# Sparse attention and an MLP mixer on one core: row-tiled score visits of three steps over six PSUM banks, with all banks handed out by one planner

## The chip, the cores and the metric

The kernel runs on one core of one Trainium2 chip. The metric is the device time of one launch in microseconds (us). The kernel before took 253.83 us in the median of three runs (253.22, 253.83, 253.84).

The engines are TensorE (PE in the profile, its weight loads PEld), VectorE (DVE), ScalarE (ACT), GpSimd (POOL) and SyncE (SP). Matmul results go to PSUM, which has eight banks of 512 fp32 values per partition; everything else lies in SBUF.

## The reference

Attention over 4 batches, 8 heads, 768 positions and 64 channels per head, with a block mask (blocks of 32: neighbours, first and last block, and three sampled blocks per row of blocks). Its output is the input of an MLP mixer, first over positions, then over channels.

```python
scores = (q @ k.T) / sqrt(64)                  # per batch and head, 768 x 768
scores = where(mask, scores, -1e9)
attn = exp(scores - max) / (sum(...) + 1e-9)
x = (attn @ v)                                 # heads side by side: 4 x 768 x 512
h = relu(x.T @ w_tok1) @ w_tok2                # over positions: 768 -> 256 -> 768
u = x + h.T
h2 = relu(u @ w_ch1) @ w_ch2                   # over channels: 512 -> 1536 -> 512
out = u + h2                                   # fp32
```

## The kernel before

All matmuls are in bf16. Two heads make a pair; there are 16 pairs (four per batch). A pair's scores are computed transposed, keys on the partitions, in nine steps: three groups of 256 queries (t) by three groups of 256 keys (jj). A step is four matmuls into one PSUM tile of two banks, one bank per head, then one exp over 128 x 1024 values on ACT, and, from pair 5 on, one product with the 0/1 mask on DVE. For pairs 0 to 4 the mask is part of the matmul (88 rows: 64 channels and 24 mask rows). From pair 5 on the matmuls have 64 rows; head 0 lies on partitions 0 to 63 and head 1 on 64 to 127, so the two heads' matmuls use different rows of the array and run side by side. Such a stretch of 64-row matmuls is called a visit here.

```python
def scores(s, done, rel):
    p, t, jj = s
    P.take("ps", rel)
    P.take("et", et_rel[s])
    ps = psS.tile([128, 2, 512], FP32, tag="ps", name=f"ps{p}_{t}_{jj}")
    n = p % NV
    for i in range(2):
        for hd in range(2):
            rows, h = (slice(0, 88), hd) if p < NT0 else (slice(64 * hd, 64 * hd + 64), 0)
            nc.tensor.matmul(                                             # L707
                out=ps[:, hd, 256 * i : 256 * i + 256],
                lhsT=ktb[n][rows, h, 256 * jj + 128 * i : 256 * jj + 128 * i + 128],
                rhs=qtb[n][rows, h, 256 * t : 256 * t + 256],
                start=(i == 0), stop=(i == 1),
            )
    ...
        nc.scalar.activation(out=et[:, :, :], in_=ps[:, :, :], func=AF.Exp, scale=0.125)   # L717
    ...
    if p >= NT0:                                                          # NT0 = 5
            nc.vector.tensor_tensor(                                      # L725
                out=ets[s][:, :, :].rearrange("k h (i q) -> k h i q", i=2),
                in0=ets[s][:, :, :].rearrange("k h (i q) -> k h i q", i=2),
                in1=free(mask[:, 2 * jj, 256 * t : 256 * t + 256], 0, [[0, 2], [S, 2], [1, 256]]),
                op=ALU.mult,
            )
```

The product with v (the "PV" matmuls, L797) uses the exp tile as weights: eight matmuls of 65 columns per step (64 channels and a column of ones, for the sum). After the three steps of a group of queries DVE takes the reciprocal of the sums (L811) and scales (L812). Then come the mixer's matmuls: over positions (L877, L902, with 256 columns), over channels (first layer L1018, 384 columns, four per tile; second layer L1047, 512 columns, twelve per tile). A first-layer tile is evicted with a relu by ACT (L839) or DVE (L841), whichever the planner finds free, a second-layer tile by DVE with an add (L1059).

The instructions' order is not found on the chip. While the kernel is being built, a planner steps through its own model of the engines and decides what PE, ACT, DVE and SP do next; streams have priorities (scores first, then PV, then transposes and mixing). An instruction is emitted when its inputs and buffers would be free. PSUM is divided among three pools: two score tiles of two banks each (`psS`), one bank for the attention output (`psO`), three banks for transposes and mixing (`psM`).

```python
psS = ctx.enter_context(tc.tile_pool(name="psS", bufs=2, space=bass.MemoryType.PSUM))
psO = ctx.enter_context(tc.tile_pool(name="psO", bufs=1, space=bass.MemoryType.PSUM))
psM = ctx.enter_context(tc.tile_pool(name="psM", bufs=3, space=bass.MemoryType.PSUM))
...
def qk_stream():
    todo = list(steps)
    while todo:
        s = todo.pop(0)
        ...                                # p < NT0: one step at a time
        visit = [s]
        if s != (NT0, 0, 0) or len(todo) % 2:
            visit.append(todo.pop(0))
        ...
        n = len(visit)
        yield (
            420.0 if n == 1 else 650.0, [e for x in visit for e in qk_deps(*x)],
            [("ps", n), ("et", n)], emit, None,
        )
```

So from pair 5 on a visit has two steps (the very first has one), and it is emitted when both score tiles are free.

Of the kernel before, what the change touches and what calls it, by code (L numbers as in the profile page):

```python
# [50 lines left out]
class Planner:  # L51
# [13 lines left out]
    def __init__(self, slots):  # L65
        self.now = 0.0
        self.free_at = {"pe": 0.0, "act": 0.0, "dve": 0.0, "sp": 0.0}
        self.streams = []
        self.ops = []
        self.count = 0  # L70
        self.slots = {tag: [Ev(0.0)] * n for tag, n in slots.items()}
        self.exp_pending = 0
# [6 lines left out]
    def op(self, engines, cost, deps, emit, prio=5, lat=60.0, tags=()):  # L79
        done = Ev()  # L80
        self.ops.append((prio, self.count, engines, cost, deps, emit, done, lat, tags))
        self.count += 1
        return done

# [7 lines left out]
    def when(self, deps, tags=()):  # L92
        t = 0.0
        for d in deps:
            if d.t is None:
                return None
            t = max(t, d.t)
        for tag, n in tags:
            ts = sorted(e.t for e in self.slots[tag] if e.t is not None)
            if len(ts) < n:  # L100
                return None
            t = max(t, ts[n - 1])
        return t
# [77 lines left out]
def kernel(  # L181
# [12 lines left out]
    nc = tc.nc  # L194
# [9 lines left out]
    NET = 7  # L204
# [7 lines left out]
    psS = ctx.enter_context(tc.tile_pool(name="psS", bufs=2, space=bass.MemoryType.PSUM))  # L212
    psO = ctx.enter_context(tc.tile_pool(name="psO", bufs=1, space=bass.MemoryType.PSUM))
    psM = ctx.enter_context(tc.tile_pool(name="psM", bufs=3, space=bass.MemoryType.PSUM))
# [10 lines left out]
    P = Planner({"ps": 2, "po": 1, "pm": 3, "et": NET, "a_t": 2, "o": 3, "rc": 2,  # L225
                 "uT": 3})
# [98 lines left out]
    idle_ps = psS.tile([128, 2, 512], FP32, tag="ps", name="ps_idle")  # L325

    def idle_mm(n=512):
        nc.tensor.matmul(  # L328
            out=idle_ps[:, 0, 0:n], lhsT=free(one[:, 0:1], 0, [[0, 128]]),
            rhs=free(one[:, 0:1], 0, [[0, n]]), start=True, stop=True,  # L330
        )
# [68 lines left out]
    def first_turn(nm, lo, n):  # L400
        t = psM.tile([128, n, 128], BF16, tag="pm", name=f"t{nm}first{lo}")
        for c in range(n):
            nc.tensor.matmul(  # L403
                out=t[:, c, :], lhsT=lay0[nm][:, lo + c, :, :].rearrange("p h d -> p (h d)"),
                rhs=ident[:, :], start=(c == 0), stop=(c == n - 1), is_transpose=True,
            )
        return t
# [8 lines left out]
    def e2_mm(t, pool, tag):  # L416
        ps = pool.tile([128, 256], FP32, tag=tag, name=f"pm_e2_{t}")
        nc.tensor.matmul(
            out=ps[R, :], lhsT=t2add[R, :], rhs=indf[:, 256 * t : 256 * t + 256],
            start=True, stop=True,  # L420
        )
        return ps
# [10 lines left out]
    e2a = e2_mm(0, psO, "po")  # L433
    first_lay(acopy, "q", 0, 2)
    qt0 = first_turn("q", 0, 2)
# [4 lines left out]
    kt0 = first_turn("k", 0, 2)  # L440
# [3 lines left out]
    kt1 = first_turn("k", 2, 4)  # L444
# [23 lines left out]
    def first_rest():  # L468
        nc.sync.dma_start(out=ktb[1][R, :, :], in_=bandrows)
        for t in (1, 2):  # L470
            box, last, rel = {}, Ev(), Ev()

            def emit(t=t, box=box, rel=rel):
                P.take("pm", rel)
                box["t"] = first_turn("q", 2 * t, 2)
# [11 lines left out]
            def emit(t=t, ebox=ebox, erel=erel):  # L487
                P.take("pm", erel)
                ebox["t"] = e2_mm(t, psM, "pm")
# [10 lines left out]
        for n in range(1, NV):  # L500
            def spread(eng, n=n):
                if n > 1:
                    nc.sync.dma_start(out=ktb[n][R, :, :], in_=bandrows)
                if eng == "dve":
                    nc.vector.tensor_copy(out=qtb[n][R, :, :], in_=qtb[0][R, :, :])
                else:
                    nc.sync.dma_start(out=qtb[n][R, :, :], in_=qtb[0][R, :, :])

# [13 lines left out]
    def mask_stream():  # L522
        box, last, rel = {}, Ev(), Ev()

        def emit():
            P.take("pm", rel)
            box["m"] = psM.tile([128, NC, 24], FP32, tag="pm", name="pm_mask")
# [88 lines left out]
    def transposes(p):  # L616
# [15 lines left out]
        for nm, bufs, there in (("k", ktb, kT_there), ("q", qtb, qT_there)):  # L632
# [6 lines left out]
            for c in range(NC):  # L639
                def emit(nm=nm, c=c, box=box, rel=rel, raw=raw):  # L640
                    if c == 0:
                        P.take("pm", rel)
                        box["t"] = psM.tile([128, NC, 128], BF16, tag="pm", name=f"t{nm}{p}")
# [52 lines left out]
    et_rel = {s: Ev() for s in steps}  # L696

    def scores(s, done, rel):
        p, t, jj = s
        P.take("ps", rel)  # L700
        P.take("et", et_rel[s])
        ps = psS.tile([128, 2, 512], FP32, tag="ps", name=f"ps{p}_{t}_{jj}")
# [12 lines left out]
        def exp(eng):  # L715
            et = sbw.tile([128, 2, 512], BF16, tag="et", bufs=NET, name=f"et{p}_{t}_{jj}")
            nc.scalar.activation(out=et[:, :, :], in_=ps[:, :, :], func=AF.Exp, scale=0.125)  # L717
            ets[s] = et
            P.exp_pending -= 1

        ev = P.op(("act",), {"act": 948.0}, [done], exp, prio=0, lat=80.0)
        alias(rel, ev)
        if p >= NT0:
            def cut(eng):
                nc.vector.tensor_tensor(  # L725
                    out=ets[s][:, :, :].rearrange("k h (i q) -> k h i q", i=2),
                    in0=ets[s][:, :, :].rearrange("k h (i q) -> k h i q", i=2),
                    in1=free(mask[:, 2 * jj, 256 * t : 256 * t + 256], 0, [[0, 2], [S, 2], [1, 256]]),
# [3 lines left out]
            ev = P.op(("dve",), {"dve": 695.0}, [ev, mask_there], cut, prio=5)  # L732
        alias(et_there[s], ev)
# [6 lines left out]

    def qk_stream():
        todo = list(steps)
        while todo:
            s = todo.pop(0)
            p, t, jj = s
            yield lambda p=p: (p, 1) in qT_there
            if p < NT0:
                done, rel = Ev(), Ev()
                yield (
                    436.0, qk_deps(*s), [("ps", 1), ("et", 1)],  # L750
                    lambda s=s, done=done, rel=rel: scores(s, done, rel), done,
                )
# [4 lines left out]
            visit = [s]  # L757
            if s != (NT0, 0, 0) or len(todo) % 2:
                visit.append(todo.pop(0))
            yield lambda p=visit[-1][0]: (p, 1) in qT_there  # L760
            evs = [(Ev(), Ev()) for _ in visit]

            def emit(visit=visit, evs=evs):
                for n, (x, ev) in enumerate(zip(visit, evs)):
                    scores(x, *ev)
                    ev[0].t = P.now + 330.0 + 230.0 * n + P.PE_LAT + P.SEM

            n = len(visit)
            yield (
                420.0 if n == 1 else 650.0, [e for x in visit for e in qk_deps(*x)],  # L770
                [("ps", n), ("et", n)], emit, None,
            )
            for x, ev in zip(visit, evs):
                if x[1:] == (2, 2):
                    alias(qk_done[x[0]], ev[0])

    def pv_stream():
        for s in steps:
            p, t, jj = s
            done = et_rel[s]  # L780

            def emit(s=s, done=done):
                p, t, jj = s
                b, pb = p // 4, p % 4
                et = ets.pop(s)
                if jj == 0:
                    rel = Ev()
                    P.take("po", rel)
                    po_of[p, t] = (
                        psO.tile([128, 2, 2, 65], FP32, tag="po", name=f"po{p}_{t}"), rel  # L790
                    )
                po, rel = po_of[p, t]
                va = vaug[p % NV]
                for i in range(2):
                    for hd in range(2):
                        for c in range(2):
                            nc.tensor.matmul(  # L797
                                out=po[:, hd, c, :],
                                lhsT=et[:, hd, 256 * i + 128 * c : 256 * i + 128 * c + 128],
# [27 lines left out]
            yield 236.0, [et_there[s], va_there[p], ones_there[p % NV]], [("po", 1)] if jj == 0 else [], emit, done  # L827
            if (t, jj) == (2, 2):
# [18 lines left out]
    def new_uT(b):  # L847
        P.take("uT", st[b]["uT_rel"])
        st[b]["uT"] = sbw.tile([128, 2, NC, 2, 128], BF16, tag="uT", bufs=3, name=f"uT{b}")
# [15 lines left out]
    def tok(b, g):  # L865
# [5 lines left out]
        for t in range(2):  # L871
            for sc in range(NC):
                def emit(t=t, sc=sc):
                    if t == 0 and sc == 0:
                        P.take("pm", rel)
                        box["pm"] = psM.tile([128, 2, 256], FP32, tag="pm", name=f"pm_tok1_{b}_{g}")
# [15 lines left out]
        for s2 in range(3):  # L892
            last, rel, ubox = Ev(), Ev(), {}
            for i in range(2):
                for t in range(2):
                    def emit(i=i, t=t, s2=s2, rel=rel, ubox=ubox):
                        if i == 0 and t == 0:
                            P.take("pm", rel)
                            ubox["pm"] = psM.tile(
                                [128, 2, 256], FP32, tag="pm", name=f"pm_tok2_{b}_{g}_{s2}"  # L900
                            )
# [21 lines left out]
    def tok_first(p):  # L923
# [5 lines left out]
        for t in range(2):  # L929
            for sc in range(NC):  # L930
                def emit(t=t, sc=sc):
                    if t == 0 and sc == 0:
                        P.take("pm", rel)
                        box["pm"] = psM.tile([128, 2, 128], FP32, tag="pm", name=f"pm_tok1_0_{p}")
# [15 lines left out]
        for s3 in range(2):  # L950
            last, rel, ubox = Ev(), Ev(), {}
            for i in range(3):
                for t in range(2):
                    def emit(i=i, t=t, s3=s3, rel=rel, ubox=ubox):
                        if i == 0 and t == 0:
                            P.take("pm", rel)
                            ubox["pm"] = psM.tile([128, 3, 128], FP32, tag="pm", name=f"pm_tok2_0_{p}_{s3}")
# [16 lines left out]
        for sc in range(NC):  # L974
            def emit(sc=sc, rel=rel, tbox=tbox):
                if sc == 0:
                    if p == 0:
                        new_uT(0)
                    P.take("pm", rel)
                    tbox["pt"] = psM.tile([128, NC, 128], BF16, tag="pm", name=f"pm_ut_0_{p}")  # L980
# [20 lines left out]
    def ch(b, pool, tag):  # L1001
# [4 lines left out]
        for cc in range(12):  # L1006
            for sh in range(2):
                last, rel, pbox = Ev(), Ev(), {}
                for dmc in range(4):
                    first = dmc == 0  # L1010
                    def emit(cc=cc, sh=sh, dmc=dmc, rel=rel, pbox=pbox):
                        if dmc == 0:
                            P.take("pm", rel)
                            pbox["pm"] = psM.tile([128, 512], FP32, tag="pm", name=f"pm_ch1_{b}_{cc}_{sh}")
# [8 lines left out]
                    tags = [("pm", 1)] if first else []  # L1023
# [16 lines left out]
        for sc, lo, n in parts:  # L1040
            last, rel, pbox = Ev(), Ev(), {}
            for cc in range(12):
                def emit(sc=sc, cc=cc, lo=lo, n=n, rel=rel, pbox=pbox):
                    if cc == 0:
                        P.take("pm", rel)
                        pbox["pm"] = psM.tile([128, DM], FP32, tag="pm", name=f"pm_ch2_{b}_{sc}_{lo}")
# [4 lines left out]
                yield n / 2.4 + 2.5, [rc_there[cc, sc // 3], ch2_there[cc // 3]], [("pm", 1)] if cc == 0 else [], emit, last if cc == 11 else None  # L1051
# [47 lines left out]
    def ch_stream():  # L1099
        for b in range(B):  # L1100
            yield from ch(b, psM, "pm")
# [88 lines left out]
```

The softmax here doesn't subtract the row's maximum and nothing guards it: scores larger than these inputs give would overflow.

## Time and profile before

One execution was profiled; its span is 253.1 us.

| engine | busy, us | share | instructions |
|---|---|---|---|
| PE (matmul) | 247.9 | 98% | 2807 |
| ACT | 177.9 | 70% | 225 |
| DVE | 167.0 | 66% | 372 |
| PEld (weight loads, beside PE) | 163.4 | 65% | 2807 |

The granted clock of TensorE is full (1.0) in the whole span. From 25 to 50 us, in pairs 0 to 4, ACT is busy for 24.75 of 25 us; from 75 to 100 us for 20.1, and DVE for 22.4. After 184 us no scores are left, and PE alone works through the rest of the mixer.

How to read it: the busy time of an engine is the union of its instructions' records. Matmuls overlap in the records and their ends are modelled, so the distance from one matmul's start to the next says more than its length. A group's line gives the source line, engine, operation, output and inputs by name with shapes, count, then busy time and mean length in ns, then the engine's idle time just before them and what ended it. A wait line reads "engine, line, waited for engine, line: total us, times, longest us". "Issue" is time for which the profile shows nothing waited for. In a timeline or in the chain of work that ended last, the first number is the start in us and the second the length.

### The profile page before, as it was taken

Reading aid. Unit: us, or ns where it says so; the run is one execution under the profiler, and the core shown is the slowest. Engines: PE = TensorE matmul, PEld = TensorE weight load, DVE = VectorE, ACT = ScalarE, POOL = GpSimd, SP = SyncE. Lnnn points to the kernel's source line nnn. Section 1 sums busy time; section 2 is a strip of 40 time slices with the busy share of each in tenths; the row PEclk is TensorE's granted clock in tenths of the full one; section 3 lists DMA queues with packets and bytes.
Section 4 is the critical chain, followed back from the end, with each engine's and each line's share of the span. In section 5 each row is a group of like instructions: output and inputs, shape, how many; then the busy total and the mean of one; then the engine's idle time right before and its main releaser. Section 6 shows DMA issues by size and latency. Waiting matters only on the chain.

```text
span 253.1 us, 6675 instructions
## 1 busy us (share of the span) xinstructions
PE 247.9 (98%) x2807; PEld 163.4 (65%) x2807; DVE 167.0 (66%) x372; ACT 177.9 (70%) x225; POOL 49.9 (20%) x86
## 2 busy tenths in 40 slices
PE   7999999999999999999999999999999999999994
PEld 3689999966666557556766765575576644566444
DVE  4885875788989888988889898888853012200222
ACT  5699999999888868778989787677665710277000
POOL 8845989477400000000000000000000000000000
PEclk9999999999999999999999999999999999999999
DMA  7999999999978531934153013114112012300132
GB/s 169 164 211 201 213 205 202 204 201 201 201 121 132 100 92 42 169 115 74 34 96 62 4 22 84 43 43 106 44 43 51 14 41 84 124 3 0 41 115 95
DMA packets 42462, 26.36 MB, mean 104 GB/s; under 512 B 23680, under 2 KB 38800, under 8 KB 42432
## 3 DMA queue, kind: packets, MB, share of 16 engines
q0 software_dynamic: 15104, 12.98, 32.4%
q1 hardware_dynamic: 26784, 12.56, 20.8%
q8 instruction: 22, 0.36, 0.6%
q10 hardware_dynamic: 544, 0.39, 0.5%
q14 instruction: 8, 0.07, 0.1%
HBM read 26.74 MB, written 6.29 MB: 131 GB/s over the span
## 4 chain that ended last, share of the span: by engine, by line
PE 96%; DMA 2%; ACT 1%; DVE 0%; SPq 0%; issue 0%
PE pm_ch L1018 25%; PE pm_ch L1047 25%; PE ps L707 19%; PE po L797 15%; PE pm_tok L902 3%; PE pm_tok L877 3%; DMA kf<-in_k_dram 2%; PE pm_tok L958 1%; PE pm_tok L935 1%; PE tk L649 1%; PE tq L649 1%; PE pm_ut L981 1%; ACT et L717 0%; PE ps_idle L328 0%; PE tkfirst L403 0%; PE tqfirst L403 0%
## 5 line engine op out<-in xcount | busy, mean ns | idle before, releaser
L717 ACT ACTIVATE et<-ps 128x1024 bf16<-128x1024 f32 x144 | 138.8, 1022 | 26.9 <-PE ps L707 25.9
L1018 PE MATMUL pm_ch<-uT,w_ch 128*128 128x384 bf16 x384 | 71.8, 326 | 0.0
L1047 PE MATMUL pm_ch<-w_ch,rc 128*128 128x512 bf16 (+2 forms) x312 | 70.4, 363 | 0.0
L725 DVE TENSOR_TENSOR et<-et,mask 128x1024 bf16<-128x1024 bf16 x99 | 63.9, 684 | 1.7 <-ACT et L717 1.7
L797 PEld LDWEIGHTS <-et 128*128 128x128 bf16 x1152 | 49.1, 97 | 15.7 <-issue 3.0
L707 PE MATMUL ps<-qtb,ktb 64*128 64x256 bf16 (+1 forms) x576 | 58.1, 273 | 0.5 <-ACT et L717 0.5
L797 PE MATMUL po<-vaug,et 128*128 128x65 bf16 x1152 | 55.4, 193 | 0.1
L839 ACT ACTIVATE rc<-pm_ch 128x384 bf16<-128x384 f32 x70 | 34.1, 493 | 26.3 <-PE pm_ch L1018 26.0
L1018 PEld LDWEIGHTS <-w_ch 128*128 128x128 bf16 x384 | 34.7, 97 | 21.4 <-issue 2.5
L1059 DVE TENSOR_TENSOR o<-pm_ch,x 128x512 f32<-128x512 f32 x23 | 15.8, 688 | 47.3 <-PE pm_ch L1047 47.2
L1047 PEld LDWEIGHTS <-rc 128*128 128x128 bf16 x312 | 27.4, 98 | 24.7 <-issue 1.5
L707 PEld LDWEIGHTS <-ktb 64*128 64x128 bf16 (+1 forms) x576 | 30.9, 96 | 15.6 <-issue 11.8
L812 DVE TENSOR_TENSOR x<-po,recip 128x256 bf16<-128x256 f32 x48 | 20.4, 424 | 1.7
L811 DVE RECIPROCAL recip<-po 128x4 f32<-128x4 f32 x48 | 8.7, 181 | 18.6 <-PE po L797 17.9
L841 DVE TENSOR_SCALAR rc<-pm_ch 128x384 bf16<-128x384 f32 x26 | 14.4, 554 | 2.8 <-PE pm_ch L1018 2.3
L910 DVE TENSOR_TENSOR x<-pm_tok,x 128x512 bf16<-128x512 f32 x18 | 12.0, 685 | 3.9 <-PE pm_tok L902 3.8
L902 PE MATMUL pm_tok<-a_t,w_tok 128*128 128x256 bf16 x72 | 10.7, 276 | 0.0
L877 PE MATMUL pm_tok<-x,w_tok 128*128 128x256 bf16 x72 | 9.7, 273 | 0.0
L902 PEld LDWEIGHTS <-w_tok 128*128 128x128 bf16 x72 | 7.6, 128 | 1.7 <-issue 1.1
L265 POOL DMA_DIRECT2D vraw<-in_v_dram x10 | 7.4, 738 | 3.3 <-DVE vaug L583 1.2
L877 PEld LDWEIGHTS <-w_tok 128*128 128x128 bf16 x72 | 6.5, 98 | 1.7 <-issue 0.8
L553 POOL COPY mask<-maskb 128x240 bf16<-128x240 bf16 (+1 forms) x18 | 7.4, 482 | 0.0
(93 smaller groups left out, 132.0 us busy)
## 6 DMA issues: line engine op xcount, KB each, us to landing
out_dram<-o SPq DMA_DIRECT2D x23, 256.0 KB, 2.0
w_ch<-in_moe_w_ch_dram POOLq DMA_DIRECT2D x8, 384.0 KB, 9.8
vraw<-in_v_dram POOLq DMA_DIRECT2D x10, 192.0 KB, 7.5
kraw<-in_k_dram POOLq DMA_DIRECT2D x9, 192.0 KB, 8.3
qraw<-in_q_dram POOLq DMA_DIRECT2D x9, 192.0 KB, 7.3
w_tok<-in_moe_w_tok_dram POOLq DMA_DIRECT2D x2, 384.0 KB, 10.3
qf<-in_v_dram POOLq DMA_DIRECT2D x4, 192.0 KB, 7.9
klay_first<-in_k_dram POOLq DMA_DIRECT2D x2, 192.0 KB, 8.3
```

The source lines that it names most:

```text
L707: nc.tensor.matmul(out=ps[:, hd, 256 * i : 256 * i + 256], lhsT=ktb[n][rows, h, 256 * jj + 128 * i : 256 * jj + 128 * i + 128], rhs=qtb[n] ...
L717: nc.scalar.activation(out=et[:, :, :], in_=ps[:, :, :], func=AF.Exp, scale=0.125)
L725: nc.vector.tensor_tensor(out=ets[s][:, :, :].rearrange("k h (i q) -> k h i q", i=2), in0=ets[s][:, :, :].rearrange("k h (i q) -> k h i q" ...
L797: nc.tensor.matmul(out=po[:, hd, c, :], lhsT=et[:, hd, 256 * i + 128 * c : 256 * i + 128 * c + 128], rhs=va[:, hd, 2 * jj + i, 0:65], star ...
L812: nc.vector.tensor_tensor(out=free(xs[b][:, pb // 2, 2 * t, 128 * (pb % 2) : 128 * (pb % 2) + 128], 0, [[64, 2], [256, 2], [1, 64]],), in0 ...
L839: nc.scalar.activation(out=o(), in_=i, func=AF.Relu)
L841: nc.vector.tensor_scalar(out=o(), in0=i, scalar1=0.0, scalar2=None, op0=ALU.max)
L877: nc.tensor.matmul(out=box["pm"][:, t, :], lhsT=w_tok1[:, sc, 128 * t : 128 * t + 128], rhs=xs[b][:, g, sc, :], start=(t == 0 and sc == 0) ...
L902: nc.tensor.matmul(out=ubox["pm"][:, i, :], lhsT=w_tok2[:, t, :, 2 * s2 + i], rhs=a_t[:, t, :], start=(i == 0 and t == 0), stop=(i == 1 an ...
L1018: nc.tensor.matmul(out=pbox["pm"][:, 0:384], lhsT=w_ch1[:, dmc, 128 * cc : 128 * cc + 128], rhs=st[b]["uT"][:, dmc // 2, 3 * sh : 3 * sh + ...
L1047: nc.tensor.matmul(out=pbox["pm"][:, 0:n], lhsT=box["rc"][:, cc, 128 * sc : 128 * sc + 128], rhs=w_ch2[:, cc, lo : lo + n], start=(cc == 0 ...
L1059: nc.vector.tensor_tensor(out=o[:, :].rearrange("p (g e) -> p g e", g=2), in0=pbox["pm"][:, :].rearrange("p (g e) -> p g e", g=2), in1=st[ ...
```

## The change

What it does:

- From pair 5 on the nine steps of a pair become three units of three steps (one group of queries each), and a visit is one unit: twelve matmuls in a row into six banks, in three pairs of two.
- The PSUM pools go. There is one PSUM tile with all eight banks, and the planner hands out bank numbers. Until the last scores of pair 4 the division is as before. From then on the scores have banks 0 to 5, emitted when all six are free, and the attention output and the mixing tiles share banks 6 and 7. Where neither is free, a free score bank is lent, if a rule (`lend`) finds that the next scores could not start soon anyway. After the last scores all eight banks serve the mixer.
- The exp tile holds a unit (three steps) and has its key blocks ahead of the heads in memory, so that one product with the mask can cover two steps: per unit one over 2048 and one over 1024 values. There are three such tiles, in place of seven of one step.
- The transposed mixer inputs (uT) have two buffers in place of three. The order of two transfers at the start of the kernel is exchanged.

What it is for: fewer changes between row-tiled matmuls and full ones, fewer instructions on DVE, and PSUM banks that serve whichever work can use them.

The diff, cut to its core ("..." marks cuts; the remaining hunks replace pool tiles by `take_bank` or `in_bank` in the same way):

```diff
+    def sets(self, tag):
+        pairs = [(0, 1), (2, 3), (4, 5)]
+        if tag == "ps":
+            return pairs[: 2 if self.shared == 0 else 3], []
+        if tag == "unit":
+            return [(0, 1, 2, 3, 4, 5)], []
+        if self.shared == 0:
+            return [(6,)] if tag == "po" else [(4,), (5,), (7,)], []
+        return [(6,), (7,)], [(n,) for n in range(6)]
...
+    def bank(self, tag, release):
+        own, lent = self.sets(tag)
+        groups = [g for g in own if self.ready(g) <= self.now]
+        if not groups:
+            assert self.shared == 2 or self.lend(tag)
+            groups = [g for g in lent if self.ready(g) <= self.now]
...
-    NET = 7
+    NET = 3
...
-    psS = ctx.enter_context(tc.tile_pool(name="psS", bufs=2, space=bass.MemoryType.PSUM))
-    psO = ctx.enter_context(tc.tile_pool(name="psO", bufs=1, space=bass.MemoryType.PSUM))
-    psM = ctx.enter_context(tc.tile_pool(name="psM", bufs=3, space=bass.MemoryType.PSUM))
+    psum = ctx.enter_context(tc.tile_pool(name="psum", bufs=1, space=bass.MemoryType.PSUM))
+    banks = psum.tile([128, 8, 512], FP32, name="banks")
...
+    CUTS = ((0, 1), (2,))
...
-            et = sbw.tile([128, 2, 512], BF16, tag="et", bufs=NET, name=f"et{p}_{t}_{jj}")
-            nc.scalar.activation(out=et[:, :, :], in_=ps[:, :, :], func=AF.Exp, scale=0.125)
+                ets[p, t] = sbw.tile(
+                    [128, 3, 2, 2, 256], BF16, tag="et", bufs=NET, name=f"et{p}_{t}"
+                )
+            nc.scalar.activation(
+                out=ets[p, t][:, jj, :, :, :].rearrange("k i h q -> k h i q"),
+                in_=ps.rearrange("k h (i q) -> k h i q", i=2), func=AF.Exp, scale=0.125,
+            )
...
+            def cut(eng, lo=group[0], n=len(group)):
+                et = ets[p, t][:, lo : lo + n, :, :, :].rearrange("k j i h q -> k (j i) h q")
                 nc.vector.tensor_tensor(
+                    out=et, in0=et,
+                    in1=free(mask[:, 2 * lo, 256 * t : 256 * t + 256], 0,
+                             [[S, 2 * n], [0, 2], [1, 256]]),
                     op=ALU.mult,
                 )
...
+    UNSEEN, LATER = 2500.0, 1800.0
+    HOLD = {"pm": 1600.0, "po": 1800.0, "ch1": 1800.0, "ch2": 4000.0}
+
+    def lend(tag):
...
+        return P.now + HOLD[tag] <= max(ts) + LATER
...
-            yield (
-                420.0 if n == 1 else 650.0, [e for x in visit for e in qk_deps(*x)],
-                [("ps", n), ("et", n)], emit, None,
-            )
+            def emit(p=p, t=t, evs=evs, exps=exps):
+                P.take("et", et_rel[p, t])
+                order = sorted((0, 2, 4), key=lambda n: P.ready((n, n + 1)))
+                for jj, (done, rel) in enumerate(evs):
+                    queue.popleft()
+                    P.banks[order[jj]] = P.banks[order[jj] + 1] = rel
+                    scores((p, t, jj), order[jj], done, rel, exps)
+                    done.t = P.now + 330.0 + 230.0 * jj + P.PE_LAT + P.SEM
+                if not queue:
+                    P.shared = 2
+
+            yield 870.0, qk_deps(p, t, 0), [("unit", 1), ("et", 1)], emit, None
...
-                                lhsT=et[:, hd, 256 * i + 128 * c : 256 * i + 128 * c + 128],
+                                lhsT=et[:, jj, i, hd, 128 * c : 128 * c + 128],
...
-        st[b]["uT"] = sbw.tile([128, 2, NC, 2, 128], BF16, tag="uT", bufs=3, name=f"uT{b}")
+        st[b]["uT"] = sbw.tile([128, 2, NC, 2, 128], BF16, tag="uT", bufs=2, name=f"uT{b}")
```

## The prediction

> **What bounds the kernel now.** I read the page first (engines, chain, groups), then the waits, then the timeline of one stretch, where the cost of a visit can be measured. The first part of the page, and the engine line of the chain that ended last:
>
> ```profile
> PE 247.9 (98%) x2807; PEld 163.4 (65%) x2807; DVE 167.0 (66%) x372; ACT 177.9 (70%) x225; POOL 49.9 (20%) x86
> ...
> PE 96%; DMA 2%; ACT 1%; DVE 0%; SPq 0%; issue 0%
> ```
>
> TensorE (PE) is busy for nearly the whole span and is nearly the whole chain. Ends of matmuls are modelled, so 98% alone does not say that it streams all the time; the distances between starts do. The chain in order of time, after the last scores:
>
> ```profile
> 192.66 10.52 PE pm_ch L1018 x64
> 203.18 15.54 PE pm_ch L1047 x72
> 218.72 15.60 PE pm_ch L1018 x96
> ```
>
> 10.52/64 = 0.164 us and 15.60/96 = 0.1625 us for a matmul with 384 columns, 15.54/72 = 0.216 us for one with 512: no gap in the tail. Now the stretch with row-tiled scores (pairs 5 to 15, from about 51 to 184 us), PE's timeline; columns are start, length, engine and line, operation, shapes, count:
>
> ```profile
> 83.10 0.59 PE L1047 MATMUL pm_ch<-w_ch,rc 128*128 128x512 bf16 x2
> 83.62 0.61 PE L707 MATMUL ps<-qtb,ktb 64*128 64x256 bf16 x8
> 84.17 0.66 PE L797 MATMUL po<-vaug,et 128*128 128x65 bf16 x16
> 84.66 0.81 PE L1047 MATMUL pm_ch<-w_ch,rc 128*128 128x512 bf16 x3
> ```
>
> Read starts against starts. Two L1047 from 83.10 would end at 83.10 + 2 x 0.216 = 83.53; the visit starts at 83.62, so 0.09 us go at its entry. The eight score matmuls (64 rows; the two heads run side by side, so four pairs) occupy 84.17 - 83.62 = 0.55 us. A pair streams 256 columns, 0.107 us by the 512-column pitch halved, so four take 0.43; 0.12 are left at the first pair and the exit. **One visit thus costs about 0.20 us beside its streaming.** Sixteen L797 then take 84.66 - 84.17 = 0.49, or 0.031 each, without a gap. The individual starts of the stretch say the same at all visits but one (at 55 us): their edges add up to some 9.4 us, and everything else that is not streaming to some 0.5 us.
>
> The waits:
>
> ```profile
> ACT et L717 <- PE ps L707: 25.9, 40, 1.6
> PEld L707 <- issue: 11.8, 36, 0.4
> PE ps L707 <- ACT et L717: 0.5, 1, 0.5
> ```
>
> ScalarE (ACT) waits for scores (25.9 us); PE waits for an exp once in the whole run. So neither ACT nor VectorE (DVE) holds PE up. The second line is the visit edge seen from the weight loads: before scores of a visit they wait for "issue", 0.3 us each, not for data.
>
> ACT's part of a visit, from both timelines:
>
> ```profile
> 86.30 0.61 PE L707 MATMUL ps<-qtb,ktb 64*128 64x256 bf16 x8
> 88.97 0.61 PE L707 MATMUL ps<-qtb,ktb 64*128 64x256 bf16 x8
> ...
> 86.73 1.94 ACT L717 ACTIVATE et<-ps 128x1024 bf16<-128x1024 f32 x2 [0.73 <-PE ps L707]
> ```
>
> The first exp starts 0.43 us after the visit, two take 1.94 (one 1.02 by the groups, so the second starts 0.92 after the first), and the next visit comes 2.67 us after the last. PE had 2.67 us of work there, ACT needed 2.37.
>
> **What the Trainium skill says.** "TensorEngine Tiling (Array Packing)", section Key Properties: changing the tiling mode drains TensorE. The trace agrees in kind: the edges of a visit (64 rows in, 128 out) cost 0.20 us, while L1047, L797 and L1018 follow each other freely. The same page, section "Gotcha 1: PSUM Pressure": row tiles write to different banks; so a step holds two banks here, and three steps six of eight. "VectorE: DVE Perf Modes", section "The perf-mode tier table": tensor_tensor in bf16 takes 1224 ns for 2048 elements; this trace has only 1024 elements (684 ns), which implies a fixed share of 2 x 684 - 1224 = 144 ns, an estimate from that page and the row. "Perfetto Trace Analysis", section "Identifying the Most-Contended Engine", warns that matmul busy time doesn't measure the headroom; hence the start distances above.
>
> **The change, part by part.**
> 1. Visits. 99 row-tiled steps (11 pairs x 9). Before: one single and 49 doubles = 50 visits. After: 33 triples. The matmuls stay 2807, of the same shapes. 17 visits less x 0.20 us = **-3.4 us**, all on PE, which sets the end.
> 2. Masking. Instead of 99 products of 1024 elements, 33 of 2048 and 33 of 1024: 33 x 0.144 = 4.8 us less on DVE (estimate, from above). DVE is not on the chain: 0 us. The first step's product now waits for the second exp, 0.92 us later, but its weights are used in a later period (in the order of the built program the mixing products of a unit come after the next visit or later): 0 us.
> 3. exp. Same 144 instructions of 1024 elements, but the output is written in runs of 256 in another order. I know no reason for another duration: 0 us. Were it slower, pairs 0 to 4 would show it (rival C).
> 4. Attention buffers: 3 of three steps for 7 of one. The first step of a unit needs the products of seven steps earlier done, as before; the later ones less: 0 us. uT from 3 to 2: the third is wanted only when the first has long been read: 0 us.
> 5. Banks. Up to pair 4 the order of PE's instructions is the same as before until the last scores of pair 4. Then the scores get banks 0 to 5 and the rest 6 and 7, plus lent ones. Two effects can cost. (a) ACT: three exps need 0.43 + 2 x 0.92 + 1.02 = 3.29 us from a visit's start. From the built order I summed PE's work from each visit to the next (0.216, 0.1625, 0.109, 0.056, 0.031 us by kind, 0.84 for a triple visit): mostly 3.5 to 4.4 us, six to ten in some, but 2.66 once and 3.09 twice. There PE would come 0.63 + 0.2 + 0.2 = 1.0 us early. But each step of a visit waits only for the exp of its own two banks, so the first two steps can run and part of the wait is taken up: I put +0.5. (b) Mixing tiles: a first-layer tile streams 4 x 0.1625 = 0.65 us and its eviction takes 0.50 (ACT) to 0.55 (DVE); with two banks, one often held by the attention output, the next tile may wait some tenths. Lending and the PV matmuls in between cover most of it; +0.3, a guess.
> 6. Tail (after the last visit): only wide matmuls at full pitch before; eight banks instead of three change nothing, since none waited.
>
> Sum: 253.83 - 3.4 + 0.5 + 0.3 = 251.2; since planner and trace left only 0.5 us beside edges before, I lean slightly to the good side: **251.0 us**, 1.1% less.
>
> **Rivals.**
> A. *The round trip to ACT becomes the bound.* For: all six banks of a unit come from one set, so no scores can be made ahead while the exps run, and 3.29 us of ACT stand against periods of 3.5. Against: before, 2.37 stood against 2.66, the same margin, without a stall; per step the round trip shrinks from 1.19 to 1.10 us. If each visit came 0.2 us late, 33 x 0.2 = 6.6 us: 257.
> B. *Bank shortage for the mixing tiles.* For: three banks of their own become one or two. Against: lent banks. 0.1 us at each of some 50 first-layer tiles in this stretch would be +5 us: about 255.5.
> C. *exp gets slower by the other layout.* In pairs 0 to 4 ACT is as full as PE (24.75 of 25 us busy between 25 and 50 us), so 50 ns on 45 exps would be +2.3 us: 253. Nothing in the trace before speaks for it.
> D. *DVE's relief pays.* It would need PE to wait for DVE now; the waits show 1.5 us in all of weight loads after a masking product, 0.2 at most each, and PE's starts show no gap there: at most some tenths.
>
> **Range and chances.** The edges are the only loss of PE that the change touches, so 253.83 - 3.4 = 250.4 is about the best; with the spread of the runs (253.22 to 253.84) the low end is 250.0. The high end, 252.9, lets A, B or C take 2.5 of the 3.4. To be faster by over 2% (below 248.8) it would have to save 5.1 us, more than there is: 0.02. Slower by over 2% (above 258.9) needs A or B at full size: 0.05. Within 2%: 0.93.
>
> **What would show it.** Right: 33 groups of twelve score matmuls, each with about 0.2 us of edges; the weight loads' "issue" wait before scores at two thirds of 11.8 us; fewer us of ACT waiting for scores; the tail at 0.1625 and 0.216 us. DVE less busy by about 5 us with nothing gained from it. Wrong by A: PE waiting for ACT at scores, in many visits. By B: gaps ahead of the first-layer or second-layer matmuls that end with an eviction on DVE or ACT. By C: exp's mean above 1022 ns and gaps before 50 us. The prediction fails if the edge is not per visit but per score matmul, or if PE stalls spread over the stretch so that span minus streaming does not fall.

## The result and the profile after

The changed kernel took **252.22 us** in the median (252.14 to 252.35) against 253.83 us before: 1.6 us less, a ratio of 0.9943 with a 95% interval of 0.9926 to 0.996. That is inside the predicted range, at a bit more than half of the predicted gain.

The first part of the page of the kernel after, with the engine line of its chain:

```profile
PE 244.2 (98%) x2807; PEld 163.6 (65%) x2807; DVE 164.3 (66%) x339; ACT 176.4 (70%) x225; POOL 49.5 (20%) x86
...
PE 95%; DVE 2%; ACT 1%; issue 1%
```

PE is still nearly the whole chain, but DVE has entered it with 2%. That is the first sign of the loss.

Two spans must not simply be subtracted: the profiles have 253.1 and 250.4 us, 2.7 apart, while the timed runs differ by 1.6. The cure is an anchor, a point up to which both programs do the same. It is the last scores of pair 4. PE's timeline of the kernel before, then that of the kernel after:

```profile
50.15 0.60 PE L707 MATMUL ps<-qtb,ktb 88*128 88x256 bf16 x4
```

```profile
49.11 0.60 PE L764 MATMUL banks<-qtb,ktb 88*128 88x256 bf16 x4
```

1.04 us of the difference had arisen before, where PE's order is the same. The profiled execution of the kernel before took 254.8 us, 0.97 over its median, and that of the kernel after 252.14, close to its own; so this part belongs to the one execution and not to the change. From the anchor to the start of the last matmul the traces have 199.56 us before and 197.93 after: **1.63 us less**, as the timed runs say. Sorting the distances between PE's starts in this stretch, each less the streaming of its matmul (0.216 us for 512 columns, 0.1625 for 384, 0.109 for 256, about 0.03 for 65):

| from the last scores of pair 4 to the end, us | before | after | difference |
|---|---|---|---|
| entries and exits of row-tiled visits (50, 33) | 9.39 | 6.43 | -2.96 |
| inside the visits, beyond 0.107 per pair of heads | one stall of 0.2, 11 ns at each first pair | 11 ns at each first pair | -0.4 |
| gaps between full matmuls, over 25 ns each | 0.47 (6) | 2.46 (9) | +2.0 |
| small scatter | 0.24 | 0.04 | -0.2 |
| sum | | | -1.6 |

After one of the 33 visits the next matmul comes 0.21 us later than after the others; the table counts this with the exits, but it is a gap of the new kind:

```profile
114.26 0.42 DVE L904 TENSOR_TENSOR x<-banks,recip 128x256 bf16<-128x256 f32 x1
114.74 0.64 PE L889 MATMUL banks<-vaug,et 128*128 128x65 bf16 x16
```

These attention (PV) matmuls start 0.06 us after the scaling of the attention output before them has ended; in the built program both outputs have the same bank, 6. Counted so, the edges fell by 3.2 us and the gaps grew by 2.2.

So the edges gave what they should, and new gaps took more than half of it back. This is the largest, as PE's and DVE's timelines of the kernel after show it (in brackets: idle time before, and what ended it):

```profile
89.09 0.83 PE L764 MATMUL banks<-qtb,ktb 64*128 64x256 bf16 x12
89.85 0.60 PE L1132 MATMUL banks<-w_ch,rc 128*128 128x512 bf16 x2
90.29 0.89 PE L889 MATMUL banks<-vaug,et 128*128 128x65 bf16 x24
91.22 0.18 DVE L903 RECIPROCAL recip<-banks 128x4 f32<-128x4 f32 x1 [0.53 <-PE banks L889]
91.44 0.42 DVE L904 TENSOR_TENSOR x<-banks,recip 128x256 bf16<-128x256 f32 x1
91.92 0.81 PE L1132 MATMUL banks<-w_ch,rc 128*128 128x512 bf16 x3 [0.73 <-DVE x L904]
92.66 0.61 PE L764 MATMUL banks<-qtb,ktb 64*128 64x256 bf16 x8
```

A triple visit, two second-layer matmuls, then the 24 PV matmuls. They end streaming at 90.29 + 24 x 0.031 = 91.03; the next second-layer tile starts at 91.92, 0.89 us later. What it waits for is DVE's scaling of the attention output (L904). That instruction writes x, which L1132 doesn't read; what it frees is the PSUM bank of the attention output. The two banks outside the scores were that one and the one of the second-layer tile just finished, which DVE evicts only after the scaling. No score bank was lent: in the built program the new tile has bank 6, which the attention output held. So TensorE stood still for a bank, although ACT, the round trip of the scores and DVE's load were in order.

The other long gaps: 0.48 us at 99 us (position mixing waits for the relu of its own middle result, by DVE), 0.21 at 105 and 0.46 at 140 us (second-layer tiles again, the latter after L904 too), and some 0.1 to 0.2 us ahead of PV matmuls. The one at 105 us ends 0.05 us after another eviction, that of the second-layer tile before it, which had the same bank in the built program:

```profile
104.46 0.69 DVE L1144 TENSOR_TENSOR o<-banks,x 128x512 f32<-128x512 f32 x1 [0.35 <-PE banks L1132]
105.20 0.81 PE L1132 MATMUL banks<-w_ch,rc 128*128 128x512 bf16 x3
```

### The profile page after: what moved, and what is told of

The parts are those of the page before. It is cut to its first block, busy times and chain, and to the rows that moved or that the text cites. A ratio compares the mean times of both kernels' runs of the same rounds, so it can differ in the third digit from the quotient of the medians.

```text
span 250.4 us, 6599 instructions
## 1 busy us (share of the span) xinstructions
PE 244.2 (98%) x2807; PEld 163.6 (65%) x2807; DVE 164.3 (66%) x339; ACT 176.4 (70%) x225; POOL 49.5 (20%) x86
## 4 chain that ended last, share of the span: by engine, by line
PE 95%; DVE 2%; ACT 1%; issue 1%
PE banks L1132 25%; PE banks L1104 24%; PE banks L764 17%; PE banks L889 14%; PE banks L970 3%; PE banks L992 3%; PE banks L705 2%; PE banks L389 2%; PE banks L1046 1%; PE banks L1024 1%; ACT et L777 1%; PE banks L464 1%; PE banks L1068 1%; DVE x L904 1%; DVE et L794 0%
## 5 line engine op out<-in xcount | busy, mean ns | idle before, releaser
L777 ACT ACTIVATE et<-banks 128x1024 bf16<-128x1024 f32 x144 | 137.0, 1025 | 25.5 <-PE banks L764 24.9
L1132 PE MATMUL banks<-w_ch,rc 128*128 128x512 bf16 (+2 forms) x312 | 70.0, 363 | 1.1 <-DVE x L904 1.0
L1104 PE MATMUL banks<-uT,w_ch 128*128 128x384 bf16 x384 | 68.5, 326 | 0.0
L794 DVE TENSOR_TENSOR et<-et,mask 128x2048 bf16<-128x2048 bf16 x66 | 61.1, 950 | 3.2 <-ACT et L777 3.1
L764 PE MATMUL banks<-qtb,ktb 64*128 64x256 bf16 (+1 forms) x576 | 54.6, 271 | 0.3 <-ACT et L777 0.3
L933 ACT ACTIVATE rc<-banks 128x384 bf16<-128x384 f32 x71 | 34.4, 495 | 23.0 <-PE banks L1104 22.5
L889 PE MATMUL banks<-vaug,et 128*128 128x65 bf16 x1152 | 50.3, 193 | 0.3
L1132 PEld LDWEIGHTS <-rc 128*128 128x128 bf16 x312 | 27.8, 98 | 27.5 <-issue 3.5
L764 PEld LDWEIGHTS <-ktb 64*128 64x128 bf16 (+1 forms) x576 | 32.0, 95 | 15.3 <-issue 12.2
L1144 DVE TENSOR_TENSOR o<-banks,x 128x512 f32<-128x512 f32 x23 | 15.8, 686 | 30.7 <-PE banks L1132 30.6
L904 DVE TENSOR_TENSOR x<-banks,recip 128x256 bf16<-128x256 f32 x48 | 20.4, 424 | 1.7
L935 DVE TENSOR_SCALAR rc<-banks 128x384 bf16<-128x384 f32 x25 | 13.7, 552 | 8.6 <-PE banks L1104 8.4
```

The source lines that it names most:

```text
L764: nc.tensor.matmul(out=ps[:, hd, 256 * i : 256 * i + 256], lhsT=ktb[n][rows, h, 256 * jj + 128 * i : 256 * jj + 128 * i + 128], rhs=qtb[n] ...
L777: nc.scalar.activation(out=ets[p, t][:, jj, :, :, :].rearrange("k i h q -> k h i q"), in_=ps.rearrange("k h (i q) -> k h i q", i=2), func= ...
L794: nc.vector.tensor_tensor(out=et, in0=et, in1=free(mask[:, 2 * lo, 256 * t : 256 * t + 256], 0, [[S, 2 * n], [0, 2], [1, 256]]), op=ALU.mult,)
L889: nc.tensor.matmul(out=po[:, hd, c, :], lhsT=et[:, jj, i, hd, 128 * c : 128 * c + 128], rhs=va[:, hd, 2 * jj + i, 0:65], start=(jj == 0 an ...
L904: nc.vector.tensor_tensor(out=free(xs[b][:, pb // 2, 2 * t, 128 * (pb % 2) : 128 * (pb % 2) + 128], 0, [[64, 2], [256, 2], [1, 64]],), in0 ...
L933: nc.scalar.activation(out=o(), in_=i, func=AF.Relu)
```

## The experiments

All are built on the changed kernel. Times are medians; each ratio is to the kernel before, run on the same chip in turn.

**1. What a change of mode costs.** One full matmul, a fraction of a visit long, is put between the first and second step of each visit, or, as a control, ahead of the visit. It writes to a bank that the next scores overwrite; everything else keeps its order.

```diff
+        if p >= NT0 and jj == 1:        # control: jj == 0
+            nc.tensor.matmul(
+                out=banks[:, bank, 0:32], lhsT=free(one[:, 0:1], 0, [[0, 128]]),
+                rhs=free(one[:, 0:1], 0, [[0, 32]]), start=True, stop=True,
+            )
```

Between the steps:

> One full-array matmul of 32 columns stands between the first and the second step of each of the 33 row-tiled visits; the planned order is otherwise that of the changed kernel (252.2 us). Edges are the cost of changing between full and row-tiled matmuls (about 0.19 to 0.20 us per pair of changes): 33 x 0.20 + 33 x 0.02 = +7 us, so 259. Rival, the cost of a visit is a wait for its first banks or a start-up of the scores and not the change of mode: +0.5 to 1 us, so 253.

Measured: 258.94 us, ratio 1.0208 (1.0192 to 1.0224); 6.7 us over the changed kernel's 252.22. Ahead of the visit:

> The same full-array matmul of 32 columns, 33 times, but ahead of each visit, where the array is in full mode anyway. If only a change of mode costs: 33 x 0.015 to 0.03 = +0.5 to 1 us over the changed kernel, so about 253. If an extra instruction at this place costs as such: as much as between the steps.

Measured: 252.30 us, ratio 0.9945 (0.9927 to 0.9963): nothing to be seen. In the trace the stretch from the anchor is 0.51 us longer than in the kernel after, 0.016 for each small matmul. The same instruction costs 0.2 us where it changes the mode and next to nothing where it doesn't. PE's timelines, first with the matmul between the steps, then ahead:

```profile
82.78 0.39 PE L769 MATMUL banks<-qtb,ktb 64*128 64x256 bf16 x4
83.11 0.19 PE L761 MATMUL banks<-one 128*128 128x32 bf16 x1
83.23 0.61 PE L769 MATMUL banks<-qtb,ktb 64*128 64x256 bf16 x8
```

```profile
81.57 0.18 PE L761 MATMUL banks<-one 128*128 128x32 bf16 x1
81.68 0.83 PE L769 MATMUL banks<-qtb,ktb 64*128 64x256 bf16 x12
```

In the first, two pairs of scores take 0.22 and so should give way at 83.00; the small matmul starts at 83.11 and the scores only 0.12 later. In the second, the visit starts 0.11 after the small matmul and then runs through. The edge belongs to the change between 64-row and 128-row matmuls, and it is paid once per change.

**2. Visits of two steps with everything else of the change.** The unit of three remains for the exp tile and the masking; the scores are emitted in twos.

```diff
-            yield 870.0, qk_deps(p, t, 0), [("unit", 1), ("et", 1)], emit, None
+            k = len(visit)              # 2, the very first 1
+            yield (
+                190.0 + 230.0 * k, [e for x in visit for e in qk_deps(*x)],
+                [("ps", k)] + [("et", 1)] * any(x[2] == 0 for x in visit), emit, None,
+            )
```

> The changed kernel's banks, lending, exp tiles and masking, but visits of two steps (50 visits, as in the kernel before). If the gain comes from the 17 visits fewer: it is lost again, +3.4 us over the changed kernel, less what its mixing stalls (2.0 us in its trace) shrink when a visit needs only four banks at once: 253.6 to 255.6. If the gain comes from the common handling of the banks: stays at about 252.2.

Measured: 253.21 us, ratio 0.9989 (0.9981 to 0.9997), 1.0 us over the changed kernel and 0.4 below the expected range. Its trace has the edges of 50 visits again (some 9.5 us) but hardly a gap (about 0.4 us in all over 25 ns; 20 of its 2807 matmul records are missing, and each is counted with its streaming time): the two effects, 3.1 and 2.0 us, nearly cancel. The common banks, the lending and the merged masking by themselves are worth next to nothing against the kernel before (0.1%).

**3. DVE's relief.** The product over two steps is given as two instructions, in the same place.

```diff
-                nc.vector.tensor_tensor(out=et, in0=et, in1=..., op=ALU.mult)      # 128 x 2048
+                for x in range(n):
+                    part = et[:, 2 * x : 2 * x + 2, :, :]
+                    nc.vector.tensor_tensor(out=part, in0=part, in1=..., op=ALU.mult)  # 128 x 1024
```

> The same order, but each masking product over two steps is given as two instructions of one step each, so that DVE has 33 instructions and some 33 x 0.14 = 4.6 us more work. If DVE is off the path: 252.2 to 252.5. If DVE's relief carried part of the gain (masking and evictions that PE waits for): +1 to 2 us, 253.2 to 254.2.

Measured: 251.91 us, ratio 0.9933 (0.9912 to 0.9954). The groups of the kernel after, and of this one (line, engine, operation, shapes, count, then busy us and mean ns):

```profile
L794 DVE TENSOR_TENSOR et<-et,mask 128x2048 bf16<-128x2048 bf16 x33 | 40.2, 1217 | 3.2 <-ACT et L777 3.1
L794 DVE TENSOR_TENSOR et<-et,mask 128x1024 bf16<-128x1024 bf16 x33 | 22.5, 682 | 0.0
```

```profile
L796 DVE TENSOR_TENSOR et<-et,mask 128x1024 bf16<-128x1024 bf16 x99 | 63.3, 683 | 0.5 <-ACT et L777 0.2
```

Two of 683 ns against one of 1217 is 149 ns per pair, close to the 144 estimated; over 33 that would be 4.9 us. But the records of instructions that follow each other on DVE overlap. The first pair of one unit in this kernel, then the same product in the kernel after:

```profile
109.00 1.29 DVE L796 TENSOR_TENSOR et<-et,mask 128x1024 bf16<-128x1024 bf16 x2
```

```profile
109.12 1.22 DVE L794 TENSOR_TENSOR et<-et,mask 128x2048 bf16<-128x2048 bf16 x1
```

That is 0.07 us for the pair, and DVE's whole busy time is 167.0 us here and 164.3 in the kernel after: the merging relieves DVE by 2.7 us, little more than half of the sum of the records. Giving them back to DVE costs no time at all. DVE's load is off the path; what brings it into the chain in the kernel after is its place, not its amount.

**4. The gaps: the lending rule.** First the other extreme, no lending while scores are left:

```diff
     def lend(tag):
         if not queue:
             return True
+        return False        # and the transposed input's second half waits for the first
```

> Visits of three steps over six banks, but nothing is lent while scores are left: the attention output and all mixing tiles have banks 6 and 7 alone. (The second half of a transposed mixer input waits for the first, which the planner needs to place it.) If the visits need the lent banks for PE to stay fed: gaps of the size of an eviction and a semaphore, 0.7 us and more, ahead of most mixing tiles, and work pushed behind the last visit: 262 to 280. If two banks were enough: 252.

Measured: 272.37 us, ratio 1.0746 (1.0725 to 1.0767). Its waits of PE, the longest first:

```profile
PE banks L890 <- DVE x L905: 8.5, 14, 1.1
PE banks L890 <- DVE x L1005: 2.0, 4, 0.8
PE banks L1109 <- DVE rc L936: 1.1, 1, 1.1
```

L890 is the PV matmul and L905 the scaling of the attention output before it, which it does not read: one attention output waits for the bank of another, 8.5 us in all. The trace has 21.6 us of gaps. Visits of three over six banks, with the two remaining banks for all else, are thus a loss of 19 us against the kernel before; the lending carries the change. How much of it the added wait of the second half costs was not tried by itself.

Then a small shift of the rule. It lends a score bank if the time for which a tile is counted to hold it ends early enough for the next scores. Two of these times were altered:

```diff
-    HOLD = {"pm": 1600.0, "po": 1800.0, "ch1": 1800.0, "ch2": 4000.0}
+    HOLD = {"pm": 1600.0, "po": 2400.0, "ch1": 1800.0, "ch2": 3000.0}
```

The changed kernel beside it, on the same chip:

> The changed kernel once more, beside the next two on one chip: 252.2 us, and in its trace again about 2 us of gaps ahead of mixing and attention matmuls, at the same places.

Measured: 252.06 us (251.6 to 252.32), ratio 0.9946 (0.9931 to 0.996), gaps of 2.46 us at the same places. And with the two numbers:

> The changed kernel with two numbers of the lending rule altered: a second-layer tile is counted to hold a bank for 3.0 us instead of 4.0 (it is lent a score bank more readily), an attention output for 2.4 instead of 1.8 (less readily). If PE's gaps of 2 us come from second-layer tiles that find no bank: they go, and the edges stay at 33 x 0.19 us, so 250.2 to 250.9. If the gaps come from late exps (a visit's round trip to ACT) or from DVE: they stay, 252.2, or grow as lent banks hold up the visits, 253 or more.

Measured: **249.56 us** (249.19 to 250.16), ratio 0.9849 (0.9831 to 0.9867): 3.9 us less than before, and 2.5 less than the changed kernel beside it, 0.6 more than expected. Edges and work are the same to 0.2 us; of the gaps 0.31 us are left. The waits of PE for evictions in the changed kernel, then PE's only wait for an exp with the two numbers:

```profile
PE banks L1132 <- DVE x L904: 1.0, 2, 0.7
...
PE banks L992 <- DVE a_t L935: 0.3, 1, 0.3
```

```profile
PE banks L764 <- ACT et L777: 0.5, 1, 0.5
```

This last one lies in the start-up, at 9.67 us. After 20 us the view lists no wait of PE for anything with the two numbers; the 0.31 us of gap stand at 214.04 us, among the first-layer matmuls of the tail. In the built program the second-layer tile at 89 us, the place of the 0.89 us gap, now has a lent bank, 4. This is the version that beats both kernels.

**5. The two numbers one by one.** Only the second-layer tiles' 3.0 us:

> Only the first of the two numbers (a second-layer tile is counted to hold a bank for 3.0 us instead of 4.0). If lending to second-layer tiles removes the bank gaps: none of 0.2 us or more is left between 80 and 150 us. But more of the second layer is then done early, and in the built order only six second-layer matmuls (1.3 us) stand between the last position mixing and the first layer that needs its transposed result, which takes about 0.9 us of adding and 4 to 5 us of transfer: one gap of about 4 us near 205 us. Together 253 to 254.5. If the gaps were not about banks: they stay, and with the tail it is 256.

Measured: 258.09 us, ratio 1.0164 (1.0133 to 1.0196), 4.6 us over the kernel before on the same chip and far over the expected range. The expected gap in the tail is there, 4.6 us where about 4 were foretold. In the order it stands where it should, after the six second-layer matmuls and the first two first-layer ones; in time it lies at 218 us and not near 205:

```profile
216.38 1.46 PE L1132 MATMUL banks<-w_ch,rc 128*128 128x512 bf16 x6
217.68 0.49 PE L1104 MATMUL banks<-uT,w_ch 128*128 128x384 bf16 x2
222.75 7.53 PE L1104 MATMUL banks<-uT,w_ch 128*128 128x384 bf16 x35 [4.59 <-DMA uT<-x]
```

But three things come on top. The bank gaps between 80 and 150 us are gone, as expected, but two others of 0.57 and 0.65 us stand at 158.7 and 159.9 us. PE's clock falls after the long gap (last section), which costs 1.7 us. With the gap in the tail, and less the gaps that are gone, this comes to 5.0 us; the stretch from the anchor is 5.1 longer than in the changed kernel. And in this profile the clock was also low in the start-up, which put the anchor 3.4 us later than in the changed kernel beside experiment 4. Only the second number:

> Only the second number (an attention output is counted to hold a bank for 2.4 us instead of 1.8). The built order keeps the places where a second-layer tile waits for a bank (2 and 3 of its matmuls around 24 of the attention product): the 0.9 and 0.2 us gaps stay, the tail has 52 second-layer matmuls as cover: 251.2 to 252.2. If the second number is what removed the gaps: 249.6.

Measured: 251.73 us, ratio 0.993 (0.9915 to 0.9945): the gaps of 0.89, 0.48 and 0.21 us are at their old places, and one of 0.57 us stands for that of 0.46. So the first number removes the bank gaps between 80 and 150 us, and with it the second keeps 28 second-layer matmuls in place of six for the wait in the tail. Neither does it alone.

## Why the prediction was right, and where not

1. *Visits, -3.4 us.* Right. The edges fell by 2.96 us (3.2 without the one gap that the sorting counts with them) and the inside of the visits by 0.4, of which 0.2 is one stall of the kernel before; experiment 1 shows that the change of mode is the cause and its cost 6.7/33 = 0.20 us, of which 0.016 are the small matmul's own. Two plans that are nearly free of gaps, with 50 and with 33 visits (experiments 2 and 4), differ by 253.21 - 249.56 = 3.65 us (3.5 by the two ratios, as they ran on different chips).
2. *Masking, 0 us.* Right in time, but the relief of DVE was put too high. A record of 2048 elements is 151 ns shorter than two of 1024 (2 x 684 - 1217, against the estimated 144), but DVE is less busy by 2.7 us and not by "about 5" (167.0 to 164.3), as the records of the single products overlap.
3. *exp, 0 us.* Right: its mean is 1025 ns after 1022. Rival C is out.
4. *Buffers, 0 us.* No wait of PE in the trace after points to the exp tiles or the transposed mixer input; not tried by itself.
5. *Banks, +0.5 and +0.3 us.* This is the term that was mis-sized: +2.0 us, or 2.2 with the gap at 114.74. Part (a) was wrong in kind. I had found the three short periods (2.66 and twice 3.09 us of work against 3.29 for three exps) and let the scores wait there for ACT. PE's wait for an exp is 0.3 us in the whole run, and that at 9.6 us, ahead of any visit. The planner had left those periods short because it had no bank to give to more work (with the altered rule of experiment 4 it fills them), and in the trace each has its gap ahead of a second-layer tile, not of the scores: 0.89, 0.21 and 0.46 us. The first and the last end with the scaling L904, the one of 0.21 with the eviction L1144. So the loss is for the most part of the kind of part (b): with the gap at 114.74 about 1.8 us of waits for a bank, beside the 0.48 us at 99 us, a wait for data. And "0.3, a guess" was too little, because I judged it by first-layer tiles. The second-layer tile is the one that matters: twelve matmuls of 0.216 us, so it holds a bank for at least 2.6 us and its eviction, and was the tile that the rule lent to least. The measured time lies in the range all the same, as the range left 2.5 us for such a loss.
6. *Tail.* Right; in the kernel after, 96 first-layer matmuls take from 215.90 to 231.50 us, 0.1625 each.

Rival A (round trip to ACT) is out, as PE waits for no exp after the start-up, and rival D by experiment 3; rival B is what happened, at some 40% of the size given to it. One of my signs was useless: the weight loads' "issue" wait before scores did not fall to two thirds but went from 11.8 to 12.2 us. The view counts idle time of the weight loads, 0.2 to 0.4 us each, in 36 of the 50 visits before and in 35 places after. This idle time contains the streaming of the wide matmul ahead of the visit (0.11 to 0.22 us) beside the edge, and is 0.05 us where PV matmuls stand ahead, as at 15 visits before; after the change every visit follows wide matmuls. Distances between starts are the measure, not this wait.

## What to carry to other kernels

Count the changes between row-tiled and full matmuls and price them by start distances; here, with PE as the bound, batching paid just that. Whatever batching takes from the other work in buffers must be paid from the rest: look for the tile that holds a buffer longest and ask where it goes when the last buffer is taken, and check the filler that covers later transfers too. Where a planner fixes the order, a small change of its rule can shift the time by more than the change under study (here 249.6 to 258.1 us by two numbers), so compare from an anchor and by sorted gaps, not by totals alone.

## What the runs showed beside that

TensorE's granted clock fell twice in the profile of experiment 5's first kernel: once in the start-up, from 8.3 to 15.1 us, and once after the gap of 4.6 us. Busy time per stretch, with the granted clock in the column ahead of the last two:

```profile
0.00:12.00 12.00, 9.35 (x45) 4.54 (x46) 7.42 (x28) 6.64 (x9) 10.93 (x24) 0.85 0.91 160
...
217.00:222.00 5.00, 1.16 (x6) 0.49 (x5) 1.28 (x2) 0.00 (x0) 0.00 (x0) 1.00 0.54 123
222.00:224.00 2.00, 1.25 (x6) 0.69 (x6) 0.00 (x0) 0.49 (x1) 0.00 (x0) 0.83 0.10 21
224.00:227.00 3.00, 3.00 (x11) 1.44 (x10) 0.00 (x0) 1.07 (x3) 0.00 (x0) 0.54 0.00 0
227.00:232.00 5.00, 5.00 (x33) 3.03 (x31) 0.00 (x0) 3.84 (x8) 0.00 (x0) 1.00 0.01 3
```

About 0.7 us after work resumed, matmuls of 384 columns followed each other by 0.320 us instead of 0.162 for some 3.4 us, then at the old pace. The second fall seems to come with every execution of that kernel: its four mean clocks are 0.978, 0.985, 0.993 and 0.993, and 3.4 us at half clock in 256 would make 0.993 (an estimate). The gaps of up to 1.28 us in the kernel without lending left the clock full. That the long gap is the cause was not tried by itself, and what lowered the clock in the start-up is open.
